# Convolution with two heads in a fourth slot, spread by DMAs, from block 8 on

## The chip, the cores and the metric

The kernel runs on one core of a Trainium2 chip. The metric is the time of one execution on the device, in microseconds (us); the kernel before was timed three times. The engines of a core are PE (TensorE: matmuls, with PEld for its weight loads), ACT (ScalarE), DVE (VectorE), POOL (GpSimd) and SP (SyncE, which here only issues DMAs).

## The reference, cut to what matters

A dynamic convolution feeds a feed-forward network with a squared ReLU:

```python
# x (8, 4096, 192), weight_gen (8, 4096, 8 heads, 7 taps); group = 192 // 8 = 24
w = softmax(weight_gen, axis=-1)
x_pad = concatenate([zeros((B, 6, D)), x], axis=1)
out = einsum('bshk,bskhg->bshg', w, unfold(x_pad))      # each token: 7 rows of x, weights per head
# then, with 32768 tokens, w_in (192, 2048), w_out (2048, 192)
h = maximum(out @ w_in, 0.0)
return h * h @ w_out
```

## The kernel before, in words

The 32768 tokens are 64 sub-blocks of 512 (L50, L51). A *block* is the unit of the schedule (L52): blocks 0 and 1 hold one sub-block each, blocks 2 to 32 two. `BLOCKS[j]` gives block j's first sub-block and their number. Everything is written out in one program order; each engine works through its own part of it in that order, and waits on semaphores where it needs another's result.

**Softmax (class `Softmax`, L169).** `weight_gen` is loaded for a part of a batch, up to 4096 tokens. It is then worked on in pieces of 8 of a partition's rows, the last piece having 6: an exp on ACT (L217, plan letter E), and on DVE a sum, a reciprocal and four products (L224, L231, L239, letter S). The finished part goes to DRAM (L253), and from there each sub-block's rows come back as tile `wr` (`wr_load`, L316). For the small parts of the first two batches the rows move within SBUF instead (`move_rows`, L526, and `wr_load_sbuf`, L321), by DMAs on SP's and POOL's queues in turn.

**Bands (`st_band`, L338, letter B).** For each sub-block DVE multiplies `wr` by a mask and gets `bd`, a banded matrix for each head over five tiles of 104 tokens (`bounds`, L66). This is the moving operand of the convolution.

**Convolution (`st_conv`, L397, letter C).** The stationary operand is `x_t`, 128 rows of x by up to 32 channels. The result has channels on partitions: the 192 channels are 3 groups k of 64, and the two sub-blocks of a block lie on partitions 0 to 63 and 64 to 127, so that there are four column tiles of 32 (`tile_position=(0, p0)`). A head has 24 channels, so that a quadrant of 32 channels takes parts of two heads. `conv_pieces` (L370) makes two passes over each quadrant for that: one writes all 32 partitions with the weights of the later head, and one then overwrites the first 8, 16 or 24 with those of the earlier. This is 3 k x 2 passes x 5 tiles x 2 halves x 2 quadrants = 120 matmuls. Two tiles `yp` of PSUM take the result, and two ACT copies (1024 columns for k = 0 and 1, 512 for k = 2) bring it into `y` (L432).

**Units (`st_unit`, L437, letter u).** A unit makes 128 of the 2048 hidden channels for a block of two sub-blocks: 6 matmuls of 64 rows (L446, two row tiles side by side) with weights `w_i` from `w_in_chunk` (L150), a ReLU on ACT (L455) and a square on DVE (L458). `w_i` holds the weights with their channels on the partitions that `y` has, and a copy with the two halves exchanged (part 1). A block has 16 units.

**Second product (`st_mm2`, L468, letter M).** It is done by quarters of 256 tokens, each in two halves of 8 of the 16 chunks; a plan's M is one half, 32 matmuls (L480). A quarter accumulates into two banks `o0` and `o1` of PSUM, of which there is one pair (`ps_o` has `bufs=1`, L85). At the end of a quarter `o_sum` (L489) brings it out: an ACT copy of the one bank (L494), then a DVE add of the other (L496). After every second quarter `o_store` sends the result out on SP. In block j the M's are those of block j-1. The first M of a quarter, which is M1, M3, M5 and M7 of a block, reuses the banks that the add after M2, M4, M6 and M8 (the last of the block before for M1) has read.

**Buffers.** Tag `h` of PSUM has three slots of two banks, in turn for `h` and `yp` (L84). `t1`, from the ReLU to the square, has 5 buffers, `g` 28, `wr` 4, `bd` 3, `x_t` 2, `y` 2.

**The order.** From block 4 on each block follows `steady` (L586), `"MuMuuu" * 3 + "MuuuMCu"`: four groups of two M and four u, and in the last one the convolution C of the *next* block, ahead of u15. `fill` places the other steps ahead of a unit of a given number: bands B of the next block at u=1 and 5 (`us`, L637), softmax pieces S mostly at u=15 and 9 (`TIMES` and the default in L626), their exps E earlier in ACT's order (`exp_time`; that for u=15 at u=8). After C the x tiles of the block after that are requested on POOL's queue (`x_load`, L302), which convert to 16 bits on the way. Blocks 0 to 3 have plans of their own (L587).

Of the kernel before, what the change touches and what calls it, by code (L numbers as in the profile page):

```python
# [9 lines left out]
def kernel(  # L10
# [26 lines left out]
    nc = tc.nc  # L37
    f32 = mybir.dt.float32
    f16 = mybir.dt.float16

    B, S, D = x.shape
    H, KK = weight_gen.shape[2], weight_gen.shape[3]
    Dff = moe_w_in.shape[1]
    Dm = moe_w_out.shape[1]
    HK = H * KK
    HP = H // 2

    P = 128
    TB = 512
    NBB = S // TB  # L50
    NSUB = B * NBB  # L51
    BLOCKS = [(0, 1), (1, 1)] + [(n, 2) for n in range(2, NSUB, 2)]  # L52
# [6 lines left out]
    RT = 64  # L59
    NK = D // RT  # L60

    NT = 5
    STEP = 104
    BASE = -24
    starts = [BASE + STEP * i for i in range(NT)]
    bounds = [0, 104, 208, 312, 416, TB]  # L66
# [5 lines left out]
    const = ctx.enter_context(tc.tile_pool(name="const", bufs=1))  # L72
# [6 lines left out]
    p_y = ctx.enter_context(tc.tile_pool(name="p_y", bufs=2))  # L79
# [4 lines left out]
    ps_h = ctx.enter_context(tc.tile_pool(name="ps_h", bufs=3, space=bass.MemoryType.PSUM))  # L84
# [3 lines left out]
    WQ = 2  # L88
    NQ = Dff // WQ
    w_i = const.tile([P, WQ, 2, NQ + NQ // 2], f16, name="w_i")  # L90
    w_o = const.tile([P, NF, Dm], f16, name="w_o")
    mask = const.tile([P, P, 2], f16, name="mask")
    swap = const.tile([P, P], f16, name="swap")
# [53 lines left out]
                )  # L147
            nc.scalar.copy(out=w_i[:, q, 1, a:b], in_=pt[:, 0 : b - a])

    def w_in_chunk(fc, slot, half):  # L150

        q, f = divmod(fc, NQ // P)
        if slot < 2:
            part, col = slot, f * P
        else:
            second, f = divmod(f, NQ // P // 2)
            part, col = int(second != half), NQ + f * P
        return w_i[RT * half : RT * (half + 1), q, part, col : col + P]
# [10 lines left out]
    class Softmax:  # L169
# [10 lines left out]
        def load(self, eng):  # L180
            r, rh = self.r, self.rh
            self.wg = wg = self.tile(p_wg, p_wg, "wg", HK, "wg8").rearrange(
                "p (r h k) -> p r h k", h=H, k=KK
# [4 lines left out]
            def src(first, count, parts):  # L188
                return bass.AP(
                    tensor=base.tensor, offset=base.offset + first * HK,  # L190
                    ap=[[r * HK, parts], [1, count * HK]],
                )
# [12 lines left out]
        def exp(self, lo, hi):  # L205

            if lo == 0:
                self.ex = self.tile(p_one, p_one, "ex", HK, "ex8").rearrange(
                    "p (r g k e) -> p r g k e", g=HP, k=KK, e=2
                )  # L210
# [57 lines left out]
    x_t, wr_t, bd_t, yp_t, y_t, g_t, h_t, t1_t, o_t, o_sb_t = ({} for _ in range(10))  # L268

    def rows(ap2d, t0, width):  # L270

        return bass.AP(
            tensor=ap2d.tensor, offset=ap2d.offset + t0 * width,
            ap=[[width, P], [STEP * width, NT], [1, width]],
        )
# [5 lines left out]
    def tile_start(j, i):  # L281

        t1 = (j % NBB + 1) * TB
        return TB - P if i == NT - 1 and t1 in ends(j // NBB) else starts[i]
# [17 lines left out]
    def x_load(j):  # L302
        x_t[j] = p_x.tile([P, NT, D], f16, name="xt")
        block_load(j, x_t[j], x[j // NBB], D, nc.gpsimd)

    def x_load_f32(j):
        x_st[j] = p_one.tile([P, (R + HALO) * HK], f32, name="x_st", tag="ex")
        block_load(
# [51 lines left out]
            op=AluOp.mult,  # L360
        )

    G = D // H
    quads = []
    for q in range(D // 32):
        ha, hb = (32 * q) // G, (32 * q + 31) // G
# [3 lines left out]
    def conv_pieces(j):  # L370
# [18 lines left out]
        else:  # L389
            for pair in zip(*halves):  # L390
                for later in (True, False):
                    for k in range(NK):
                        for s, i, half, a, b, base in pair:
                            for q in (2 * k, 2 * k + 1):
                                yield later, s, i, q, half, a, b, base

    def st_conv(j):  # L397

        n = BLOCKS[j][1]
        th = n * TB // 2  # L400
        per = 1024 // th
        y = p_y.tile([P, NK, TB], f16, name="y")
        y_t[j] = y
        yps = [
            ps_h.tile([P, 2 * TB], f32, name="yp", tag="h") for _ in range(-(-NK // per))
        ]
        for later, s, i, q, half, a, b, base in conv_pieces(j):
            lo = bounds[i]
            hi = lo + (STEP if tile_start(s, i) == starts[i] else bounds[i + 1] - lo)
            _, ha, hb, pre = quads[q]  # L410
            m, h = (32, hb) if later else (pre, ha)
            bd = bd_t[s][:, H * lo : H * hi].rearrange("p (g c e) -> p g e c", g=HP, e=2)
            p0 = RT * half + 32 * (q % 2)
            k = q // 2
            col = th * (k % per) - base
            nc.tensor.matmul(  # L416
                out=yps[k // per][p0 : p0 + m, col + a : col + b],
                lhsT=x_t[s][:, i, 32 * q : 32 * q + m],
                rhs=bd[:, h // 2, h % 2, a - lo : b - lo],
                start=True,  # L420
                stop=True,
                skip_group_check=True,
                tile_position=(0, p0),
            )
        for n, yp in enumerate(yps):
            k0, k1 = n * per, min((n + 1) * per, NK)

            copies = ((k0, k1, nc.scalar.copy),)
            if j == 0:
                copies = ((0, 2, nc.scalar.copy), (2, NK, nc.vector.tensor_copy))  # L430
            for a, b, copy in copies:
                copy(  # L432
                    out=y[:, a:b, 0:th],
                    in_=yp[:, (a - k0) * th : (b - k0) * th].rearrange("p (k c) -> p k c", c=th),
                )

    def st_unit(j, u):  # L437

        th = BLOCKS[j][1] * TB // 2
        per = TB // th  # L440
        h = ps_h.tile([P, 2, TB], f32, name="h", tag="h")
        for jj in range(per):
            for slot in range(NK):
                for half, r0 in enumerate((0, RT)):
                    k = slot ^ half if slot < 2 else slot
                    nc.tensor.matmul(  # L446
                        out=h[:, half, jj * th : (jj + 1) * th],
                        lhsT=w_in_chunk(u * per + jj, slot, half),
                        rhs=y_t[j][r0 : r0 + RT, k, 0:th],
                        start=(jj == 0 and slot == 0), stop=(slot == NK - 1),  # L450
                        skip_group_check=True,
                        tile_position=(r0, 0),
                    )
        t1 = p_t1.tile([P, 2, TB], f16, name="t1")
        nc.scalar.activation(out=t1, in_=h, func=ActF.Relu)  # L455
        g = p_g.tile([P, 2, TB], f16, name="g")
        g_t[(j, u)] = g
        nc.vector.tensor_tensor(out=g, in0=t1, in1=t1, op=AluOp.mult)  # L458
# [56 lines left out]
    with nc.allow_low_precision("fp16 matmul pipeline"), tc.manual_schedule():  # L515
# [30 lines left out]
        s0, s1, s2 = parts[:3]  # L546
# [31 lines left out]
        for q in range(4):  # L578
# [5 lines left out]


        steady = "MuMuuu" * 3 + "MuuuMCu"  # L586
        plans = {  # L587
            0: "B1 X1 u u u E1 S1 u C u u u u",
            1: "L3 u u B2 M E2 B3 u M E2 u u S2 u M u C u S2 M",
# [33 lines left out]
        for n, s in enumerate(parts[4:], 4):  # L623
            b, f = s.b, s.fb
            k = n - min(m for m, p in enumerate(parts) if p.b == b)
# [8 lines left out]
        for j in range(len(plans), NBLK - 1):  # L634
            a = BLOCKS[j + 1][0]
            small = [p for p in parts if p.fb <= j + 1][-1].r == FIRST
            us = {4: (7, 9), 6: (7, 9)}.get(j, (5, 9) if small else (1, 5))  # L637
            for n, u in enumerate(us):
                at(j, u, "B", a + n)
        for j in range(len(plans), NBLK):  # L640
            plan, u = [], 0
            for step in steady:
                if step == "u":
                    plan += [f"{kind}{n}" for kind, n in fill.get((j, u), ())]
                    u += 1
                plan.append(step)
            plans[j] = " ".join(plan)
# [49 lines left out]
        for j in range(NBLK):  # L697
            if j + 2 < NBLK:
                load_rows(j + 2)
            u = 0  # L700
            for step in plans[j].split():
                kind, n = step[0], int(step[1:] or 0)
                if kind == "u":
                    st_unit(j, u)
                    u += 1
                elif kind == "M":
                    next(mm2)
                elif kind == "C" and j + 1 < NBLK:
                    st_conv(j + 1)
                    if j == 0:  # L710
                        x_load(3)
                    elif j + 2 < NBLK:
                        for k in range(BLOCKS[j + 2][0], sum(BLOCKS[j + 2])):
                            x_load(k)
                elif kind == "E":
                    parts[n].exp(*next(parts[n].exps))
                elif kind == "S":
                    soft(parts[n])
                elif kind == "B":
                    st_bands(n)  # L720
                elif kind == "L":
                    parts[n].load(nc.sync)
                elif kind == "X":
                    x_cast(n, nc.vector.tensor_copy)


        j = NBLK - 1
# [44 lines left out]
```

The softmax here doesn't subtract the row's maximum and nothing guards it: scores larger than these inputs give would overflow.

## Time and profile before

| what | value |
|---|---|
| timed runs | 747.28 us median of 3 (746.94 to 747.54) |
| profiled execution | span 746.6 us, which lies 0.7 us below that median; it is an execution of its own |
| PE | 738.7 us busy (99%) |
| ACT, DVE | 624.4 us (84%), 621.7 us (83%) |
| POOL | 89.3 us (12%) |
| L480 matmuls of the second product | x8032, 385.4 us |
| L446 matmuls of the units | x3168, 380.3 us |
| L416 matmuls of the convolution | x3864, 52.0 us |
| L432 ACT copies of the convolution | 1024 columns x31, mean 1012 ns; 512 columns x32, mean 592 ns |
| L348 band, 128x4160 | x42, mean 2314 ns |
| L300 x loads on POOL | 240 KB, 6.2 us from issue to landing |

How to read it: each number of a row is of the one profiled execution. Matmuls in different tiles of the array run side by side, so their durations add up to more than they occupy; the chain of waits and the starts of matmuls show what a stretch costs. In the chain, "PE o L480 x32" is one M, "PE h L446 x6" a unit (x18 three in a row), "PE yp L416" a convolution. "Issue" in the chain is time in which nothing was waited for that the profile shows. In a list of instructions the bracket at the end of a line is the engine's idle time before it and what ended that.

### The profile page before, as it was taken

The page shows a single profiled execution, that of the slowest core. Times are in us where ns is not written, and L with a number is a line of the kernel's source. Part 1 is how long each engine was busy: PE and PEld are TensorE (multiplying, and loading weights), DVE is VectorE, ACT ScalarE, POOL GpSimd, SP SyncE. Part 2 cuts the span into 40 slices and gives each one's busy share as a digit, 9 for nine tenths or more (in the row PEclk, how much of TensorE's full clock was granted, in tenths as well). Part 3 has the DMA queues.
Part 4 walks back from the last instruction along what each step waited for, and adds up shares of the span by engine and source line. Part 5 has one row for each costly group of instructions (what it writes and reads, how often), then busy time and mean ns, then how long its engine had stood idle before and what let it go on. Part 6 is the DMA issues. An engine that isn't in the chain of part 4 may idle for free.

```text
span 746.6 us, 33289 instructions
## 1 busy us (share of the span) xinstructions
PE 738.7 (99%) x15106; PEld 556.1 (74%) x15106; DVE 621.7 (83%) x1002; ACT 624.4 (84%) x755; POOL 89.3 (12%) x130
## 2 busy tenths in 40 slices
PE   8999999999999999999999999999999999999998
PEld 4767777777777778777877777777778777777787
DVE  5999998998889888887889888898888987677853
ACT  4998888898888888888888888888888888888884
POOL 7322220101101100011000110001100011000000
PEclk9999999999999999999999999999999999999999
DMA  7745444436554234643245442265341354432312
GB/s 214 121 97 119 80 86 99 99 72 139 94 118 80 73 59 80 139 79 73 40 80 139 94 72 56 48 139 108 59 80 46 59 108 80 60 70 52 53 46 65
DMA packets 122169, 64.81 MB, mean 87 GB/s; under 512 B 83849, under 2 KB 118636, under 8 KB 121516
## 3 DMA queue, kind: packets, MB, share of 16 engines
q1 hardware_dynamic: 77708, 45.66, 22.3%
q0 software_dynamic: 44176, 16.93, 20.5%
q8 instruction: 118, 1.93, 1.1%
q14 instruction: 23, 0.19, 0.1%
q10 hardware_dynamic: 144, 0.10, 0.0%
HBM read 48.61 MB, written 28.70 MB: 104 GB/s over the span
## 4 chain that ended last, share of the span: by engine, by line
PE 91%; DVE 4%; DMA 2%; ACT 2%; issue 1%; DVEq 0%; ACTq 0%; SPq 0%
PE o L480 43%; PE h L446 42%; PE yp L416 6%; DVE bd L348 2%; DVE g L458 1%; ACT t L455 1%; DMA vd<-v_big 1%; DMA wr<-v_first 1%; DMA wg<-in_weight_gen_dram 0%; DVE v_big L239 0%; ACT ex L217 0%; DVE o_sb L496 0%; DVE ssum L224 0%; DVE rcp L231 0%; DVE v_first L239 0%
## 5 line engine op out<-in xcount | busy, mean ns | idle before, releaser
L455 ACT ACTIVATE t<-h 128x1024 f16<-128x1024 f32 x512 | 496.7, 1026 | 64.5 <-PE h L446 63.9
L458 DVE TENSOR_TENSOR g<-t 128x1024 f16<-128x1024 f16 x512 | 334.1, 687 | 99.1 <-ACT t L455 96.4
L480 PEld LDWEIGHTS <-g 64*128 64x128 f16 (+1 forms) x8032 | 352.5, 94 | 54.2 <-issue 3.8
L480 PE MATMUL o<-w_o,g 64*128 64x192 f16 (+1 forms) x8032 | 385.4, 243 | 0.2
L446 PE MATMUL h<-y,w_i 64*128 64x512 f16 (+1 forms) x3168 | 380.3, 370 | 1.9 <-ACT t L455 0.8
L446 PEld LDWEIGHTS <-w_i 64*128 64x128 f16 x3168 | 162.5, 94 | 117.5 <-issue 5.2
L348 DVE TENSOR_TENSOR bd<-wr,mask 128x4160 f16<-128x4160 f16 (+3 forms) x89 | 149.3, 1701 | 4.2 <-DMA wr<-v_first 4.2
L300 POOL DMA_DIRECT2D xt<-in_x_dram x62 | 51.6, 836 | 445.6 <-PE yp L416 422.7
L494 ACT COPY o_sb<-o 128x384 f32<-128x384 f32 x129 | 62.2, 482 | 33.7 <-PE o L480 33.7
L496 DVE TENSOR_TENSOR o_sb<-o,o_sb 128x384 f32<-128x384 f32 x123 | 68.2, 554 | 8.2 <-ACT o_sb L494 5.6
L432 ACT CAST y<-yp 128x1024 f16<-128x1024 f32 (+1 forms) x64 | 47.9, 799 | 15.1 <-PE yp L416 15.0
L416 PE MATMUL yp<-bd,xt 128*32 128x104 f16 (+8 forms) x3864 | 52.0, 208 | 0.7 <-DVE bd L348 0.3
L416 PEld LDWEIGHTS <-xt 128*32 128x32 f16 (+3 forms) x3864 | 46.2, 92 | 7.1 <-issue 6.4
L239 DVE TENSOR_TENSOR v_big<-ex,rcp 128x112 f16<-128x112 f32 (+1 forms) x136 | 27.3, 264 | 2.1 <-DMA vd<-v_big 0.9
L217 ACT ACTIVATE ex<-wg 128x448 f32<-128x448 f32 (+2 forms) x44 | 27.2, 618 | 2.1 <-DMA wg<-in_weight_gen_dram 2.1
L224 DVE TENSOR_REDUCE ssum<-ex 128x64 f32<-128x448 f32 (+2 forms) x44 | 26.1, 593 | 2.6 <-ACT ex L217 2.6
L231 DVE RECIPROCAL rcp<-ssum 128x64 f32<-128x64 f32 (+2 forms) x44 | 23.7, 539 | 1.5
L290 POOL DMA_DIRECT2D xt<-in_x_dram x7 | 3.8, 548 | 137.1 <-PE yp L416 137.1
L330 POOL DMA_DIRECT2D wr<-v_first x31 | 16.8, 559 | 16.1 <-DVE v_first L239 15.9
L544 PE MATMUL wp<-warm 128*128 128x512 f16 x39 | 10.7, 440 | 1.3 <-DVE warm L536 1.3
L544 PEld LDWEIGHTS <-warm 128*128 128x128 f16 x39 | 4.2, 111 | 7.1 <-issue 2.6
L239 DVE TENSOR_TENSOR v_first<-ex,rcp 128x112 f16<-128x112 f32 (+1 forms) x48 | 9.1, 255 | 0.3
(25 smaller groups left out, 28.7 us busy)
## 6 DMA issues: line engine op xcount, KB each, us to landing
out_dram<-o_sb SPq DMA_DIRECT2D x63, 384.0 KB, 3.0
xt<-in_x_dram POOLq DMA_DIRECT2D x42, 240.0 KB, 6.2
wg<-in_weight_gen_dram SPq DMA_DIRECT2D x4, 1064.0 KB, 8.3
xt<-in_x_dram POOLq DMA_DIRECT2D x20, 192.0 KB, 5.4
wr<-vd SPq DMA_DIRECT2D x38, 80.0 KB, 3.9
vd<-v_big SPq DMA_DIRECT2D x5, 512.0 KB, 5.5
wg<-in_weight_gen_dram SPq DMA_DIRECT2D x5, 392.0 KB
wg<-in_weight_gen_dram SPq DMA_DIRECT2D x3, 616.0 KB, 4.5
```

Source lines behind the costliest of these rows:

```text
L217: nc.scalar.activation(out=self.ex[:, lo:hi].rearrange("p r g k e -> p (r g) k e"), in_=self.wg[:, lo:hi].rearrange("p r (g e) k -> p (r g ...
L239: eng.tensor_tensor(out=bass.AP(tensor=v.tensor, offset=v.offset + lo * H * SL + lo % SL * 2 + g * SL * 2, ap=[list(v.ap[0]), [H * SL + 2, ...
L300: eng.dma_start(out=dst[:, first:last], in_=ap)
L348: nc.vector.tensor_tensor(out=bd_t[j][:, H * lo : H * (lo + len(tiles) * n)].rearrange("p (g m c) -> p g m c", g=shape[1], c=2 * SL), in0= ...
L416: nc.tensor.matmul(out=yps[k // per][p0 : p0 + m, col + a : col + b], lhsT=x_t[s][:, i, 32 * q : 32 * q + m], rhs=bd[:, h // 2, h % 2, a - ...
L432: copy(out=y[:, a:b, 0:th], in_=yp[:, (a - k0) * th : (b - k0) * th].rearrange("p (k c) -> p k c", c=th),)
L446: nc.tensor.matmul(out=h[:, half, jj * th : (jj + 1) * th], lhsT=w_in_chunk(u * per + jj, slot, half), rhs=y_t[j][r0 : r0 + RT, k, 0:th], ...
L455: nc.scalar.activation(out=t1, in_=h, func=ActF.Relu)
L458: nc.vector.tensor_tensor(out=g, in0=t1, in1=t1, op=AluOp.mult)
L480: nc.tensor.matmul(out=oo[:, cc * Dm : (cc + 1) * Dm], lhsT=g[r0 : r0 + n, cc * P : (cc + 1) * P], rhs=w_o[r0 : r0 + n, fc, :], start=(fc ...
L494: nc.scalar.copy(out=o_sb, in_=o[0][:, c])
L496: nc.vector.tensor_tensor(out=o_sb, in0=o[1][:, c], in1=o_sb, op=AluOp.add)
```

## The change

It has five parts, of which the second to fourth concern blocks 8 to 32 alone (`FIRST_SPREAD = 8`).

1. A second set of weights `w_p`, as large as `w_i`, is loaded by `load_w_spread`, called in block 3 after C and its x loads: 16 loads from DRAM and 2 copies within SBUF, all on POOL's queue. Its rows are in a new order: each group of 32 partitions has the 24 channels of one head, and in its last 8 partitions a third of the channels of head 6 or 7.
2. `st_conv_spread` takes the place of `st_conv`. Heads 0 to 5 have a quadrant each in slots k = 0 to 2, heads 6 and 7 have a fourth slot. No quadrant has two heads, so that one pass is enough: 4 slots x 5 tiles x 2 halves x 2 = 80 matmuls. Slots 3 and 2 go to the first `yp`, 0 and 1 to the second; each is copied by one ACT copy of 1024 columns. Four DMAs on SP's queue then spread the 24 channels of the fourth slot over the free last 8 partitions of the quadrants of slots 0 to 2.
3. `st_unit` takes its weights from `w_p`. It has 6 matmuls as before.
4. From block 7 to 32 the plan is `steady_spread`, `"MuMuuu" * 2 + "MCuMuuu" + "MuMuuu"`: C stands in the third group, ahead of u8, and the fourth group is like the others. The bands of the next block are placed at u=1 and 4.
5. `G = D // H` is moved up in the file.

```diff
+    G = D // H
+    SPREAD = H - 2
+    FIRST_SPREAD = 8
...
+    w_p = const.tile([P, WQ, 2, NQ + NQ // 2], f16, name="w_p")
...
+    def load_w_spread():
+
+        def rows(head, k=None):
+            a = moe_w_in[G * head : G * (head + 1)]
+            return a if k is None else a.rearrange("(r k) c -> k r c", k=NK)[k]
+
+        for e in (0, 1):
+            for k in range(NK):
+                for a, n, src in (
+                    (0, G, rows(2 * k + e)), (G, RT // 2 - G, rows(SPREAD + e, k))
+                ):
+                    if k < 2:
+                        p0 = RT * k + 32 * e + a
+                        nc.gpsimd.dma_start(
+                            out=w_p[p0 : p0 + n, :, 0, 0:NQ],
+                            in_=src.rearrange("r (q c) -> r q c", q=WQ),
+                        )
+                    else:
+                        for half in (0, 1):
+                            p0 = RT * half + 32 * e + a
+                            nc.gpsimd.dma_start(
+                                out=w_p[p0 : p0 + n, :, 0, NQ:],
+                                in_=src.rearrange("r (q h c) -> h r q c", q=WQ, h=2)[half],
+                            )
+        for r0, r1 in ((0, RT), (RT, 0)):
+            nc.gpsimd.dma_start(out=w_p[r0 : r0 + RT, :, 1], in_=w_p[r1 : r1 + RT, :, 0])
+
-    def w_in_chunk(fc, slot, half):
+    def w_in_chunk(w_i, fc, slot, half):
...
+    def st_conv_spread(j):
+
+        s0, n = BLOCKS[j]
+        y = p_y.tile([P, NK + 1, TB], f16, name="y")
+        y_t[j] = y
+        for ks in ((NK, NK - 1), (0, 1)):
+            yp = ps_h.tile([P, 2, TB], f32, name="yp", tag="h")
+            k0 = min(ks)
+            for k in ks:
+                for i in range(NT):
+                    a, b = bounds[i], bounds[i + 1]
+                    for half in (0, 1):
+                        s = s0 + half
+                        hi = a + (STEP if tile_start(s, i) == starts[i] else b - a)
+                        bd = bd_t[s][:, H * a : H * hi].rearrange(
+                            "p (g c e) -> p g e c", g=HP, e=2
+                        )
+                        for e in (0, 1):
+                            head = 2 * k + e
+                            p0 = RT * half + 32 * e
+                            c0 = min(G * head, D - 32)
+                            nc.tensor.matmul(
+                                out=yp[p0 : p0 + 32, k - k0, a:b],
+                                lhsT=x_t[s][:, i, c0 : c0 + 32],
+                                rhs=bd[:, head // 2, e, 0 : b - a],
+                                start=True,
+                                stop=True,
+                                skip_group_check=True,
+                                tile_position=(0, p0),
+                            )
+            nc.scalar.copy(out=y[:, k0 : k0 + 2], in_=yp)
+        for p0 in range(0, P, 32):
+            head = SPREAD + p0 // 32 % 2
+            r0 = p0 + G * head - min(G * head, D - 32)
+            nc.sync.dma_start(out=y[p0 + G : p0 + 32, 0:NK], in_=y[r0 : r0 + G, NK])
+
     def st_conv(j):
 
+        if j >= FIRST_SPREAD:
+            return st_conv_spread(j)
...
+        w = w_p if j >= FIRST_SPREAD else w_i
...
-                        lhsT=w_in_chunk(u * per + jj, slot, half),
+                        lhsT=w_in_chunk(w, u * per + jj, slot, half),
...
         steady = "MuMuuu" * 3 + "MuuuMCu"
+        steady_spread = "MuMuuu" * 2 + "MCuMuuu" + "MuMuuu"
...
             us = {4: (7, 9), 6: (7, 9)}.get(j, (5, 9) if small else (1, 5))
+            if j + 1 >= FIRST_SPREAD:
+                us = (1, 4)
             for n, u in enumerate(us):
                 at(j, u, "B", a + n)
         for j in range(len(plans), NBLK):
             plan, u = [], 0
-            for step in steady:
+            for step in steady_spread if j + 1 >= FIRST_SPREAD else steady:
...
                         for k in range(BLOCKS[j + 2][0], sum(BLOCKS[j + 2])):
                             x_load(k)
+                    if j == 3:
+                        load_w_spread()
```

## The prediction

> **What bounds the kernel now.** I read the busy times first, then the chain of waits, then the chain, VectorE and POOL in order of time.
>
> ```profile
> PE 738.7 (99%) x15106; PEld 556.1 (74%) x15106; DVE 621.7 (83%) x1002; ACT 624.4 (84%) x755; POOL 89.3 (12%) x130
> PEclk9999999999999999999999999999999999999999
> PE 91%; DVE 4%; DMA 2%; ACT 2%; issue 1%; DVEq 0%; ACTq 0%; SPq 0%
> ```
>
> PE is busy and at full clock throughout, and carries 91% of the chain. Work taken from PE counts one for one, if nothing makes PE wait instead. One steady block of the chain (start us, us, what):
>
> ```profile
> 370.96 1.51 PE yp L416 x110
> 372.47 0.76 PE h L446 x6
> 373.23 1.32 PE o L480 x32
> 374.55 0.65 PE h L446 x6
> 375.19 1.32 PE o L480 x32
> 376.51 1.94 PE h L446 x18
> 378.46 1.32 PE o L480 x32
> ```
>
> A convolution (C) takes 1.51 us, a unit (u) 0.65, a half quarter of the second product (M) 1.32. The next C starts 22.54 us later, at 393.50: a block is 1.51 + 16 x 0.65 + 8 x 1.32, and 0.11 lost after C (0.76 against 0.65). I call the start of a block's first M time T (373.23 here). M3 then starts at T+5.23, M5 at T+10.46.
>
> VectorE in the same block (start us, us):
>
> ```profile
> 372.35 0.61 DVE L224 TENSOR_REDUCE ssum<-ex 128x64 f32<-128x448 f32 x1
> ...
> 374.51 0.69 DVE L458 TENSOR_TENSOR g<-t 128x1024 f16<-128x1024 f16 x1
> 376.29 0.69 DVE L458 TENSOR_TENSOR g<-t 128x1024 f16<-128x1024 f16 x1 [1.08 <-ACT t L455]
> 377.06 0.56 DVE L496 TENSOR_TENSOR o_sb<-o,o_sb 128x384 f32<-128x384 f32 x1
> 377.53 2.31 DVE L348 TENSOR_TENSOR bd<-wr,mask 128x4160 f16<-128x4160 f16 x1
> 379.76 2.49 DVE L458 TENSOR_TENSOR g<-t 128x1024 f16<-128x1024 f16 x4
> 382.29 0.56 DVE L496 TENSOR_TENSOR o_sb<-o,o_sb 128x384 f32<-128x384 f32 x1
> 382.76 2.31 DVE L348 TENSOR_TENSOR bd<-wr,mask 128x4160 f16<-128x4160 f16 x1
> ```
>
> The L496 add is the last reader of an output bank of the second product. There is one pair of banks, so the first M of the next quarter cannot start its second matmul before it. Both bands now stand right behind an add, and the adds end at T+4.4 and T+9.6, some 0.8 us before M3 and M5 need them. From the starts, one piece after the other costs 0.63 for a square g, 0.47 for an add, 2.23 for a band. A softmax piece of 8 rows costs 2.1 (372.35 to the g that follows it), one of 6 rows 1.65 (the three of 80.68 to 82.33).
>
> That this wait is real shows in block 4 (counted from 0), the one where a band stands before u7 and thus ahead of an add, in the chain:
>
> ```profile
> 93.47 0.68 DVE g L458
> 94.15 0.48 DVE o_sb L496
> 94.63 0.04 issue
> 94.67 1.48 PE o L480 x31
> ```
>
> PE starts 31 of the 32 matmuls of that M only 0.05 us after the add's end.
>
> [...]
>
> **The change, part by part.**
>
> *Conv matmuls.* 3 column groups x 2 passes x 5 tiles x 2 halves x 2 = 120 become 4 slots x 5 x 2 x 2 = 80, over the same four column tiles: 20 rounds for 30. 10 x 47 = 0.47 us less per conv, for blocks 8 to 32: 25 x 0.47 = **-11.8 us**. [...] The units keep their matmul count.
>
> *Second evacuation.* ACT copies 128x1024 twice (1.01 each) instead of 1024 and 512 (0.59): +0.42 on ACT, 25 times. ACT has gaps of 0.2 to 0.75 us before most units; on PE this counts only below.
>
> *The bands move from u=(1,5) to (1,4).* This is the heart of it. At u=4 the second band stands after M3 and ahead of u4's square and of M4's add. The first still stands after M2's add. VectorE's row from T is then: add2, band, g1 g2 g3, band, g4, add4. And since C no longer stands before u15, the softmax piece at u=15 comes behind g14, at T+1.35 (u13 ends at T-1.29; its ACT pass and the next take 0.92 each, g14 starts at T+0.73), where it used to start at T-0.9. So: piece 1.35 to 3.43, g15 to 4.06, g0 to 4.69, add2 to 5.16 (its end 5.24 just meets M3), band to 7.39, three g to 9.27, band to 11.50, g4 to 12.12, add4 ends 12.68. M5's second matmul is due at T+10.50 and gets 12.73: **2.2 us of stall a block**. With a 6-row piece before it 1.75; without any (add2 at T+3.83 as today) 11.83, 1.4. I take these; a g or band is known to 0.05, the position of the piece to 0.3, so 1.9 to 2.5.
> Bands of the plan run in blocks 7 to 31. Blocks 8 to 26 follow a piece: 8, 10 to 14, 16, 17, 18, 20, 21, 22, 24, 25, 26 one of 8 rows (15 x 2.2 = 33), and 9, 15, 19, 23, with 27, one of 6 (5 x 1.75 = 8.75). Block 7 (its piece at u=0): 1.75. Blocks 28 to 31: 4 x 1.4 = 5.6. Block 11 has a piece at u=0 as well, and M3 waits too: 1.65. Sum **+50.8 us**.
>
> *C in the third group.* Behind C on ACT stand two copies, the exp of u=8 (0.53), u8's pass, then M6's copy; on VectorE g8 and add6. C at 0: copies 0.67 to 2.5, exp to 3.05, pass to 4.05, g8 to 4.75, add6 ends 5.25; PE reaches M7 at 1.05 + 0.76 + 1.32 + 1.94 = 5.07. About 0.2 us of stall in the 20 blocks with an exp, 7 to 26: **+4 us** (0 to 8).
>
> *The four spread DMAs a block (SP).* SP has only M4's store ahead of them, which is over by then. From C: copies end at 2.6, four issues at 0.4 to 0.7, landing 3 to 4 us later (the small row loads take 2.9 to 3.9): about 8.5. The first unit of the next block is 8 units, 4 Ms and C later, 1.05 + 5.3 + 5.3 = 11.6. Hidden, 3 us to spare: 0. If the cover went, each us late would be 25 us. The waits themselves on PE: 0 to 0.1 a block, I take 0.
>
> *w_p's load, in block 3.* 16 loads and 2 copies go on POOL's queue ahead of the row moves of block 4, which stand there now as:
>
> ```profile
> 82.70 2.13 POOL L330 DMA_DIRECT2D wr<-v_first  x4 [1.76 <-DVE v_first L239]
> ```
>
> The loads start at 80.9; at 0.55 to 0.8 us an issue (what POOL's rows show) the last is out at 90 to 93.5, lands about 5.5 later, the copies wait for that and take 1.2, the four row DMAs 2.1 and land 3.1 later: 101 for 90.56, where the band of block 4 starts now. VectorE is blocked, and M6's add, which M7 waits for, is behind that band: **+10 us** once (4 if the loads issue at 0.3, 15 if they are slow and PE's clock drops for a window). w_p itself has four blocks to arrive.
>
> *x loads* go out earlier with C: 0. For block 8 there are some 12 us against 6.2 to land.
>
> *Sum.* -11.8 + 50.8 + 4 + 10 = +53.0. The profile's span is 746.6; the median of the runs is 747.28, 0.7 more, and I add to that: **800 us**.
>
> **Rivals.** (1) *Forecast*, the adds behind the bands: 800; its terms give 36 to 70, 783 to 817. (2) *VectorE absorbs the piece*: it lies early enough that every block pays 1.4: 25 x 1.4 = 35, -11.8 + 35 + 10 = 781. For: 83% busy leaves VectorE gaps. Against: the order in its queue. (3) *The gain comes through*, ending on the other side: 735.5 with the one-off hidden, 745.5 with it. Mechanism: M5 is not held by M4's add. It decides from the point where add4 ends before T+10.5, so VectorE would have to be 2.2 us quicker there. For: PE hardly waits at all today, 0.2 us before L480. Against: block 4. (4) *Spread DMAs land late*, by 1 us past their 3 us: 825. For: four small DMAs in a row on one queue. Against: nothing else is due there. (5) *Conv does not shrink*, the round being set by something other than the stream: 812. [...]
>
> **How the numbers follow.** Forecast 0.67, (2) 0.13, (3) 0.10, (4) 0.06, (5) 0.04. The range 774 to 818 holds (1), (2) and (5), and leaves out (3) and (4). About 0.2% is what a measurement of this kernel can tell from no change. Faster 0.08 and same 0.02 come from (3), slower 0.90 from the rest.
>
> **What would show it.** Right: conv of about 1.05 us in the chain; DVE o_sb L496 releasing PE o in each block's third group for 1.4 to 2.2 us; block time near 24.4 us; PE below 94% busy; the band of block 4 waiting for row DMAs near 100 us. Wrong: blocks of 22.1 us, or PE h waiting for the spread DMAs, or M1 and M3 rather than M5 waiting.

## The result: 814 us, slower by 9%

| | before | changed |
|---|---|---|
| median (runs) | 747.29 us (4) | 814.47 us (4: 813.68 to 815.51) |
| ratio | 1 | 1.0898, 95% interval 1.0882 to 1.0913 |
| span of the profiled execution | 746.6 us | 812.3 us |

The forecast was slower, 800 us (774 to 818), and the time lies in the range. The page of the changed kernel:

```profile
PE 744.2 (92%) x14106; PEld 552.4 (68%) x14106; DVE 617.9 (76%) x1002; ACT 634.6 (78%) x755; POOL 99.0 (12%) x148
```

PE has 1000 matmuls less (25 x 40) and is busy 92% of the span, where it was 99%. VectorE's work is what it was; only its order and PE's differ. The waits of PE in the changed kernel (engine and line, waited for: us in total, times, longest):

```profile
PE o L549 <- DVE o_sb L565: 43.3, 27, 10.1
PE o L549 <- DVE g L527: 16.8, 20, 0.9
```

Before, the list of PE's waits has neither. One block of the changed kernel, where L549 is an M, L515 a unit, L448 the convolution. PE (start us, us), from M1 at 409.37 on:

```profile
411.33 1.38 PE L549 MATMUL o<-w_o,g 64*128 64x192 f16 x28
413.63 0.34 PE L549 MATMUL o<-w_o,g 64*128 64x192 f16 x4 [0.92 <-DVE g L527]
...
420.98 0.24 PE L549 MATMUL o<-w_o,g 64*128 64x192 f16 x1
422.47 1.48 PE L549 MATMUL o<-w_o,g 64*128 64x192 f16 x31 [1.25 <-DVE o_sb L565]
423.88 1.11 PE L448 MATMUL yp<-bd,xt 128*32 128x104 f16 x80
```

And VectorE in the same block:

```profile
410.91 0.61 DVE L255 TENSOR_REDUCE ssum<-ex 128x64 f32<-128x448 f32 x1
...
412.89 1.28 DVE L527 TENSOR_TENSOR g<-t 128x1024 f16<-128x1024 f16 x2
414.52 0.56 DVE L565 TENSOR_TENSOR o_sb<-o,o_sb 128x384 f32<-128x384 f32 x1 [0.34 <-ACT o_sb L563]
414.99 2.31 DVE L379 TENSOR_TENSOR bd<-wr,mask 128x4160 f16<-128x4160 f16 x1
417.23 1.89 DVE L527 TENSOR_TENSOR g<-t 128x1024 f16<-128x1024 f16 x3
419.03 2.32 DVE L379 TENSOR_TENSOR bd<-wr,mask 128x4160 f16<-128x4160 f16 x1
421.26 0.69 DVE L527 TENSOR_TENSOR g<-t 128x1024 f16<-128x1024 f16 x1
421.87 0.55 DVE L565 TENSOR_TENSOR o_sb<-o,o_sb 128x384 f32<-128x384 f32 x1
```

This is the row that the prediction gave: add2, band, three g, band, g4, add4. M5 starts its first matmul at 420.98 and its second at 422.47, 0.05 us after add4 ends at 422.42. New against the prediction is the wait at the top. 28 of M2's 32 matmuls start in time, and the four of its last chunk come 1.14 us late (14 pairs of 0.083 after 411.33 would be 412.49). They need g15 of the block before, which stands behind the softmax piece of 410.91.

The conv itself does what was said: its matmuls start over 0.91 to 0.96 us (1.62 in block 12, at half clock), for 1385 ns before. By the distance from one convolution to the next, read off the starts of matmuls, in us:

| interval | before | changed |
|---|---|---|
| block 4 | 22.90 | 35.31 |
| after a piece of 8 rows (8, 10, 13, 14, 16 to 18, 20 to 22, 24 to 26) | 22.53 to 22.61, but 22.70 in 13 and 22.81 in 16 | 24.98 to 25.05 |
| after a piece of 6 rows (9, 15, 19, 23, 27) | 22.55 to 22.56 | 24.57 to 24.60 |
| without a piece (28 to 31) | 22.54 to 22.55, but 22.99 in 28 | 23.57 to 23.64 |
| 11 and 12 | 22.53, 22.87 | 26.62, 25.86 |

Block 4 gives 12.4 of the 65.7 us by which the span grew, the intervals from the convolution of block 8 to that of block 32 52.5, and the rest, where C moves within a block and at the end, about 1. Those 24 intervals hold 24 x 0.46 = 11.0 us of gain, so the waits in them, with a stretch of slow clock in block 12 (granted 0.50 for 3.4 us), cost 63.5 us.

In block 4 VectorE's band waited for the row DMAs on POOL, and M7 for the add behind it. POOL, VectorE and PE there:

```profile
94.01 1.24 POOL L179 DMA_DIRECT2D w_p<-w_p  x2 [3.74 <-DMA w_p<-in_moe_w_in_dram]
95.23 2.12 POOL L361 DMA_DIRECT2D wr<-v_first  x4
100.13 1.89 DVE L379 TENSOR_TENSOR bd<-wr,mask 128x3328 f16<-128x3328 f16 x1 [9.86 <-DMA wr<-v_first]
103.75 2.71 PE L549 MATMUL o<-w_o,g 64*128 64x192 f16 x31 [10.07 <-DVE o_sb L565]
```

The M of 103.75 takes 2.71 us for the usual 1.5: PE's clock had gone to half (the mean granted clock from 100 to 105 us is 0.50).

### The profile page after: what moved, and what is told of

It is laid out like the page before. It is cut to its first block, busy times and chain, and to the rows that moved or that the text cites. A ratio compares the mean times of both kernels' runs of the same rounds, so it can differ in the third digit from the quotient of the medians.

```text
span 812.3 us, 31504 instructions
## 1 busy us (share of the span) xinstructions
PE 744.2 (92%) x14106; PEld 552.4 (68%) x14106; DVE 617.9 (76%) x1002; ACT 634.6 (78%) x755; POOL 99.0 (12%) x148
## 5 line engine op out<-in xcount | busy, mean ns | idle before, releaser
L524 ACT ACTIVATE t<-h 128x1024 f16<-128x1024 f32 x512 | 497.1, 1029 | 63.5 <-PE h L515 50.7
L549 PE MATMUL o<-w_o,g 64*128 64x192 f16 (+1 forms) x8032 | 399.0, 243 | 61.3 <-DVE o_sb L565 43.3
L549 PEld LDWEIGHTS <-g 64*128 64x128 f16 (+1 forms) x8032 | 352.6, 94 | 128.9 <-issue 64.2
L515 PE MATMUL h<-y,w_p 64*128 64x512 f16 x2400 | 295.7, 377 | 0.0
L515 PEld LDWEIGHTS <-w_p 64*128 64x128 f16 x2400 | 125.9, 94 | 86.9 <-issue 0.4
L457 ACT CAST y<-yp 128x1024 f16<-128x1024 f32 x50 | 48.2, 1015 | 48.3 <-PE yp L448 48.3
L515 PE MATMUL h<-y,w_i 64*128 64x512 f16 (+1 forms) x768 | 84.1, 354 | 1.8 <-ACT t L524 0.8
L515 PEld LDWEIGHTS <-w_i 64*128 64x128 f16 x768 | 41.1, 95 | 25.8 <-issue 4.9
L448 PE MATMUL yp<-bd,xt 128*32 128x104 f16 (+1 forms) x2000 | 29.0, 212 | 0.0
L448 PEld LDWEIGHTS <-xt 128*32 128x32 f16 x2000 | 25.1, 97 | 4.1 <-issue 4.1
L262 DVE RECIPROCAL rcp<-ssum 128x64 f32<-128x64 f32 (+2 forms) x44 | 23.7, 539 | 1.5
L500 ACT CAST y<-yp 128x512 f16<-128x512 f32 (+2 forms) x14 | 10.4, 788 | 4.1 <-PE yp L484 4.1
```

What stands on the lines that cost most here:

```text
L448: nc.tensor.matmul(out=yp[p0 : p0 + 32, k - k0, a:b], lhsT=x_t[s][:, i, c0 : c0 + 32], rhs=bd[:, head // 2, e, 0 : b - a], start=True, sto ...
L457: nc.scalar.copy(out=y[:, k0 : k0 + 2], in_=yp)
L515: nc.tensor.matmul(out=h[:, half, jj * th : (jj + 1) * th], lhsT=w_in_chunk(w, u * per + jj, slot, half), rhs=y_t[j][r0 : r0 + RT, k, 0:th ...
L549: nc.tensor.matmul(out=oo[:, cc * Dm : (cc + 1) * Dm], lhsT=g[r0 : r0 + n, cc * P : (cc + 1) * P], rhs=w_o[r0 : r0 + n, fc, :], start=(fc ...
```

## The experiments

The theory: three places in VectorE's and POOL's order hold PE, namely the second band ahead of M4's add, the softmax piece ahead of g15, and the load of `w_p` ahead of the row moves. The rival: the place of the convolution and its two evacuations cost the time, or the spread convolution itself does. In a line of PE's waits below, the numbers are us in total, times, longest. The first four experiments and the one with the convolution ahead of u15 were timed once each; the differences read from their times are 10 us and more.

**Bands back at u=(1,5).**

```diff
-                us = (1, 4)
+                us = (1, 5)
```

> The changed kernel with the bands at u=(1,5) again, all else kept. Theory A (VectorE's order: M4's add stands behind the second band, and M5 waits for it): M5's wait of 1.4 us a block goes, and the second band, now behind M4's add, ends some 0.1 to 0.4 us after PE reaches the convolution, so that a smaller wait of the convolution for bd takes its place; about 31 us less than the changed kernel, 783 us. The waits in M2 and M7 stay. Theory B (it is the place of the convolution, three PSUM slots and two evacuations before u8, that stalls PE): no change, 814 us.

Measured: 778.72 us (the kernel before on the same chip 746.97).

```profile
PE o L549 <- DVE o_sb L565: 12.3, 2, 11.9
```

The waits for an add fall from 27 to 2: block 4's, and 0.35 us at M3 of block 11. The 20 waits for g15 stay as they were, 16.8 us in all. Blocks without a piece take 22.26 us for 23.6: the 1.4 of M5 is gone, and 0.2 has come in the convolution, whose matmuls now start over 1.10 us for 0.93 because the second band ends late. The gain is 36 us, for 31 expected; M5's extra wait in block 11 and block 12's slow clock are gone too (mean granted clock 0.993 for 0.991).

**The load of `w_p` in block 5.**

```diff
-                    if j == 3:
+                    if j == 5:
                         load_w_spread()
```

> The changed kernel with the load of w_p called in block 5 instead of block 3, when no row move follows on POOL's queue. Theory A (the row moves of block 4 stood behind the load on POOL, the band waited for them, and M7 for the add behind the band; PE's clock then fell for 10 us): block 4 goes back from 35.3 to 22.9 us, so 12.4 us less, 802 us, and the half clock from 98 to 109 us is gone. Theory B (the load's traffic or descriptors slow the core wherever it is): the stall moves to block 6, 814 us.

Measured: 803.89 us.

```profile
PE o L549 <- DVE o_sb L565: 32.9, 26, 2.0
```

The wait of 10.1 us is gone from the list. Block 4 takes 22.92 us; half clock there is gone (mean granted clock 0.996 for 0.991); nothing of the stall comes back in block 6 (22.85). The time is 1.9 us above the 802 expected; in this run the convolution of block 4 already starts 1.9 us later (77.49 for 75.56), ahead of either place of the load. The one-off is a matter of what was queued behind the load, not of its traffic.

**The softmax piece at u=8.**

```diff
                 for j, u in times:
-                    at(*exp_time(j, u), "E", n)
-                    at(j, u, "S", n)
+                    late = j + 1 >= FIRST_SPREAD and u == 15
+                    at(*((j, 4) if late else exp_time(j, u)), "E", n)
+                    at(j, 8 if late else u, "S", n)
```

> The changed kernel with the softmax piece of u=15 moved to u=8, right behind the convolution (its exp to u=4), in blocks 7 and later. Theory A (at u=15 the piece delays g15, for which the last chunk of M2 waits, and add2): M2's wait of about 1 us goes, M7's 0.3 too since no exp stands before u8's pass; M5's 1.4 stays. 2.9 of stall become 1.45 in 15 blocks, 2.5 become 1.45 in 5, block 11 keeps its piece at u=0: about 28 us less, 786 us. Theory B (the piece has no part in it, VectorE has gaps enough): 814 us.

Measured: 786.28 us.

```profile
PE o L549 <- DVE o_sb L565: 42.6, 26, 9.7
```

The waits for g are gone from the list, all 20, and nearly all blocks take 23.55 to 23.66 us, whether a piece comes before them or not (11, with its piece at u=0, takes 24.25, and 29 takes 23.86). That is 22.08 and the 1.5 of M5 alone.

**Only the bands, in the kernel before.**

```diff
             us = {4: (7, 9), 6: (7, 9)}.get(j, (5, 9) if small else (1, 5))
+            if j + 1 >= 8:
+                us = (1, 4)
```

> The kernel before with one edit: bands at u=(1,4) for the bands of block 8 and later. Theory A: M4's add ends at T+11.85 where M5 is due at T+10.5, so 1.4 us of stall in each of 25 blocks, a little more in blocks 7 and 11: 783 us. Theory B (the order alone costs nothing, it needs the convolution in the third group): 747 us.

Measured: 787.54 us, 40.6 above the kernel before on that chip, by this edit alone.

```profile
PE o L480 <- DVE o_sb L496: 32.6, 25, 1.6
```

25 waits in 25 blocks. Most blocks take 24.01 to 24.11 us for 22.55, that is 1.5 each and not 1.4; blocks 7 and 11, with a piece at u=0, 24.4; five others 24.14 to 24.62. The convolution's place and form have no part in it.

**The three edits together**, and **the same without the spread DMAs** (`pass` in their place in `st_conv_spread`: the part of heads 6 and 7 is left out of the result):

> The changed kernel with the three edits together: bands at u=(1,5), load of w_p in block 5, softmax piece at u=8. Theory A (the three waits add up to the whole loss): blocks 8 to 31 take 22.25 to 22.4 us (22.07 of PE work and a wait of the convolution for the second band of about 0.2), against 22.5 before: 739 to 743 us, below the kernel before. Theory B (the spread convolution has a cost of its own that the waits hid): above 750 us.

> The kernel of the three edits without the four DMAs of each block that spread heads 6 and 7, so that their part of the sum is left out. If the DMAs are hidden, as the prediction has it: the same time within 0.2%. If they or their waits cost PE time: faster by 0.1 us a block or more, 2.5 us or more in all.

Measured (medians of 4): 741.48 us, ratio to the kernel before 0.9908 (95% interval 0.9892 to 0.9924), and 741.70 us, ratio 0.9909 (0.9892 to 0.9925). The three waits make up the loss, and without them the change is a gain of 0.9%. What PE still waits for in the first of the two is the second band:

```profile
PE yp L448 <- DVE bd L379: 1.1, 5, 0.3
```

Blocks take 22.1 to 22.7 us. The list has 5 such waits; by the matmul starts the convolution takes 0.1 us and more longer than 0.94 in most blocks. The DMAs cost nothing that can be measured here: from the convolution of block 8 to that of block 32 both kernels take 535.95 us.

**The convolution ahead of u15 again**, with the bands at u=(1,5) and the late load of `w_p`:

```diff
-        steady_spread = "MuMuuu" * 2 + "MCuMuuu" + "MuMuuu"
+        steady_spread = steady
```

> The changed kernel with bands at u=(1,5), load of w_p in block 5, and the convolution in the fourth group ahead of u15, where it stood before. Theory A (the spread DMAs need some 8.5 us from the start of the convolution, and only u15 and M1 would lie over them, 3.1 us): the first unit of each block waits some 5.3 us, 25 times: 133 us over 735, 868 us, and more, up to 950, if PE's clock falls in each of these waits. Theory B (the DMAs are quick enough for any place): 736 to 745 us.

Measured: 947.75 us.

```profile
PE h L515 <- DMA y<-y: 146.9, 29, 6.5
```

The first unit of each block waits for the spread DMAs, 5.95 us in the one after the convolution of 412.31: C starts at 412.31, the DMAs are issued from 414.98 to 417.81, and the unit starts at 421.48, which is 9.2 us after C where the prediction had 8.5. PE's clock falls to half there: in the three stretches of 5 us from 415 to 430 the granted clock is 0.95, 0.50 and 0.87, which is 6.8 us at half. The mean of the run is 0.911; by my estimate from these figures that is some 24 such falls in the 25 blocks, and they make the rest of the loss: blocks take 30.3 to 31.0 us. So the cover that the DMAs have in the third group is real, and worth some 200 us.

**The convolution behind u8**, all else as in the three edits, but the two pieces at u=8 and 9:

```diff
-        steady_spread = "MuMuuu" * 2 + "MCuMuuu" + "MuMuuu"
+        steady_spread = "MuMuuu" * 2 + "MuCMuuu" + "MuMuuu"
...
-                    at(*exp_time(j, u), "E", n)
-                    at(j, u, "S", n)
+                    late = j + 1 >= FIRST_SPREAD and u in (9, 15)
+                    at(*((j, 4) if late else exp_time(j, u)), "E", n)
+                    at(j, {9: 8, 15: 9}[u] if late else u, "S", n)
```

> Bands at u=(1,5), load of w_p in block 5, and the convolution one unit later than in the change, behind u8 (M u C M u u u in the third group), so that the second band is over when PE comes to it; the softmax pieces of u=9 and 15 at u=8 and 9, their exps at u=4. Theory A: no wait is left but a few tenths in one block of four: 22.1 us a block, 736 to 738 us. If the convolution behind u8 finds no free PSUM slot, or M7 has to wait for its add: 740 us or more.

Measured (median of 4): 738.31 us, ratio 0.9867 (0.9849 to 0.9885), the fastest kernel here.

```profile
PE o L549 <- DVE o_sb L565: 0.5, 3, 0.2
```

Most blocks take 22.07 to 22.10 us: PE's work and nothing else. Blocks 15, 19, 23 and 27, where two pieces meet, take 22.37, and blocks 8, 10 and 11, which have the three waits of the list, 22.49 to 22.52. The time is 0.3 us above the upper end of what was expected.

**The old convolution in that order** (`st_conv` and `w_i` throughout, `w_p` not loaded):

> The kernel with the convolution behind u8 and all its placements, but with the convolution of before (120 matmuls, one evacuation of 1024 and one of 512 columns, no spread DMAs) and the weights w_i; w_p isn't loaded. What is left between the two is the spread convolution itself. Theory A (its gain is the 0.46 us of matmuls, 25 times): 11.6 us above that kernel, 22.55 us a block, no difference from the kernel before within 0.3%. Theory B (a good part of the gain over the kernel before comes from the new order): 742 us or less.

Measured (median of 5): 752.00 us, ratio 1.0047 (1.0034 to 1.0061). Between the two lie 13.7 us, more than the 11.6. Of the 24 blocks from 8 on, 14 take 22.52 to 22.57, which is 0.46 above the spread convolution's. The rest is in ten blocks of 22.7 to 23.7, in most of which PE waits for nothing that the profile names:

```profile
PE o L547 <- issue: 2.6, 5, 0.9
PE yp L482 <- issue: 1.7, 3, 1.0
```

What these eight stretches are was not shown, and why the kernel before has hardly any stays open. The order alone brings no gain (with these stretches the time is 0.5% longer); the gain over the kernel before is the matmuls.

## Why the prediction was right, point by point

The time alone does not part the forecast (800 us) from rival (5), in which the convolution doesn't shrink (812 us). The starts of the convolution's matmuls do: 0.92 us for 1.385.

*PE bounds, and its work counts one for one.* Right: with the waits out, blocks of 22.09 us stand for 22.55.

*Conv matmuls, -11.8 us.* Right: 0.46 us a conv, for 0.47. The 47 ns a round in the sum can be read off the trace of the kernel before: 120 matmuls, four side by side, start over 1385 ns, so that four starts take 1385 / 119 x 4 = 47 ns. In the changed kernel 80 start over 0.91 to 0.96 us, 46 to 48 ns for four.

*The band ahead of M4's add.* Right in mechanism and place, shown from both sides: put alone into the kernel before it costs 40.6 us, taken out of the changed one it gives back 36. Without a piece it costs 1.45 to 1.5 for 1.4.

*The softmax piece.* Here is what failed in part. The prediction had the piece start at T+1.35 and g15 end at T+4.06 and let both pass on to add2, band and add4 alone: 2.2 us at M5. The piece starts at T+1.54, and g15 has a reader of its own that was missed: the last chunk of M2, due at T+3.1. PE loses 1.14 us there. Since M5 is then due later, its own wait is 1.45 and not 2.2, and M7's is about 0.3 for 0.2. The sum is 2.9 a block for 2.4 with an 8-row piece, 2.5 for 1.95 with one of 6: about 10 us of the 14 by which the forecast was short. That the sum came so near is in part luck: M5's wait is 0.75 less than forecast, and M2's, which was not in the sum, more than fills the gap. The rival in which VectorE absorbs the piece fell with it.

*The load of `w_p`.* Right: a wait of 10.07 us for 10. The clock's fall, left to the range, added 2.3: no trace from before the change shows one in its steady part, and in the changed kernel the granted clock was 0.50 from 98.5 to 108.8 us.

*The spread DMAs cost nothing.* Right, within what the two kernels can tell; the spare time was about 2.4 us (11.6 less the 9.2 of the run with C ahead of u15) and not 3.

*C in the third group, 0.2 at M7.* About 0.3 in the changed kernel. With the piece and the exp moved it is gone.

*The gain comes through* needed VectorE 2.2 us quicker ahead of M5. Nothing of the kind happened; it came through only where the order was changed.

## What to carry to other kernels

On a PE-bound kernel look, for every step on another engine that is moved, at which instruction behind it in that queue hands something back to PE, and when PE is due there: here a small add that frees a PSUM bank, a square read by the last chunk of a product, and four small DMAs behind a weight load, none of them near the top of a list of busy times. Trace each delayed result to all its readers, not just to the next instruction in the queue. A saving of 12 us turned into a loss of 67 by placement, and into a gain of 10 us with the same instructions placed anew.

## What the runs showed of the hardware

The forecast counted no loss of clock for its waits of 1.4 to 2.2 us a block. In the changed kernel one wait of 1.97 us, in block 11, was followed by half clock. The second row below has a stretch, its length, the busy times of PE, PEld, DVE, ACT and POOL, the mean granted clock (0.50), and two figures of the DMAs:

```profile
271.66 1.69 PE L549 MATMUL o<-w_o,g 64*128 64x192 f16 x29 [1.97 <-DVE o_sb L565]
274.00:276.00 2.00, 2.00 (x68) 1.41 (x59) 0.00 (x0) 1.46 (x2) 0.36 (x1) 0.50 0.04 8
```

The half clock lasted 3.4 us, the convolution in it took 1.62 us for 0.92, and the interval 0.9 more. It came in the kernel with the late load of `w_p` too, whose longest such wait is 2.0 us (mean granted clock 0.996, for 1.000 of the kernel before). In the changed kernel it never came after the waits of 1.24 to 1.31 us of the other blocks, nor after one of 1.60 in block 7. And it did not come after a wait of 1.94 us, almost as long, in block 11 of the kernel with the piece at u=8:

```profile
265.71 0.51 PE L549 MATMUL o<-w_o,g 64*128 64x192 f16 x8 [1.94 <-DVE o_sb L565]
265.60:269.00 3.40, 3.29 (x122) 2.69 (x122) 3.33 (x9) 1.17 (x2) 0.46 (x1) 1.00 0.39 120
```

So two waits of nearly the same length differ. In the trace of the changed kernel the clock falls at 98.54 and 272.62 us and is back at 108.78 and 276.03, so that its changes lie 10.24, 163.84 and 3.41 us apart, multiples of 3.41. Cut into slices of 3.41 us from these changes on, that trace has 3.41 us of idle PE in the slice ahead of the first fall, 1.97 (269.20 to 272.62) in the one ahead of the second, and at most 1.45 in any other slice at full clock between the start-up and the last matmuls. My estimate from this one trace is that the idle time within a slice counts; no run was made to test it.
